# Gated scan attention and an MoE-like feed-forward on one core: attention as closed visits to TensorE, and another start

## The chip, the cores and the metric

The kernel runs on one core of a Trainium2 chip. The metric is the device time of one execution in microseconds. Before the change it is 642.63 us, the median of three runs that lie between 638.91 and 644.26. Engines are named as in the profile: PE is TensorE, DVE VectorE, ACT ScalarE, POOL GpSimd, SP SyncE, which issues all DMAs here (its queue is SPq). PEld is the loading of weights into PE.

## The reference

Four batches of eight heads, 768 positions, head size 48. Each head keeps a complex state of 48 x 48, turned and damped at each position by a gate that is normalised to a magnitude of at most 0.999; what it reads with q is x, 3072 tokens by 384, and x goes through two matrix products with an activation between them:

```python
mag = np.sqrt(a_re * a_re + a_im * a_im)
scale = np.minimum(mag, 0.999) / (mag + 1e-06)
a_re_n, a_im_n = (a_re * scale, a_im * scale)
for t in range(S):
    ar, ai = (a_re_n[:, :, t, :, None], a_im_n[:, :, t, :, None])
    new_re = ar * S_re - ai * S_im
    new_im = ar * S_im + ai * S_re
    kv = np.einsum('bhd,bhe->bhde', k[:, :, t], v[:, :, t])
    S_re, S_im = (new_re + kv, new_im)
    y[:, :, t] = np.einsum('bhd,bhde->bhe', q[:, :, t], S_re)
x = y.transpose(0, 2, 1, 3).reshape(3072, 384)

h = x @ w_in                                   # 384 x 2048
g = np.where(h >= 1, h, np.where(h <= -1, 0.0, (h + 1) ** 2 / 4))
out = g @ w_out                                # 2048 x 384
```

q, k, v and the gates are float32, w_in and w_out are float64.

## The kernel before

**Stages.** The scan is made as attention over chunks: positions are cut into 12 units of 256 (three a batch), each of two chunks of 128. `gates(u)` loads a unit's gates (tile `ai`) and its k and q (`kq`), makes logarithms, angles, sines and decays of them on ACT (one line for all its passes, L396) and DVE, runs a summing scan over the positions on DVE, and ends with two products on DVE, `turn(X, 0)` and `turn(KQ, 1)` (L521), which write k and q turned by the gates into `x` and `kq`. After each turn `spread` moves the result by DMA into the head tiles `hd0`, `hd1`, `hd2` (`hd<-x`, `hd<-kq` at L287), of which there is one set.

`attend(u)` then does, for each chunk and each of two groups of four heads: scores on PE (`sc`, L670), which DVE multiplies by the triangular mask (`am`, L679); transposes of k on PE (`tp`, L613), copied by ACT (`kT`, L624); products of kT with the values on PE (`dp`, L633), added by DVE into the running state (`st`); and values on PE (`yp`, L705 from the state, L713 from the masked scores), copied by ACT into the block's tile `xr` and its rest rows `ys` (L727, L734, L759). After a block's last chunk six DMAs move `ys` into `xr`. In the traces a fp32 matmul is two records.

`moe(blk)` takes two units, 512 tokens, at a time: six blocks. `split` makes `xH` (ACT, L784) and `xL` (DVE, L791) from `xr`, a coarse and a fine part. For each of 16 slices of the hidden size nine matmuls of 512 columns make `h` (L812, in two banks by turns), ACT makes s = Relu(h/2 + 1/2) (L835), DVE g = max(h, s) (L842) and g = min(s, 1) * g (L849), ACT rounds it to `gh` (L855), DVE keeps the difference `gl` (L859), and three slices later nine matmuls add into the three output banks `o0` to `o2` (L872). "MoE" in the texts is all this.

**Weights.** `weights` loads 16 tiles of float64 bits (768 KB each), makes float32 values of them in three integer steps on DVE (L329, L338, L347), casts a coarse part on ACT (L353) and subtracts on DVE for the fine part (L357). Ahead of these ACT sums |w| (L314) and Relu(bound - |w|) (L321) of each tile into `wsum`: the range check. At the end flags are made of all sums; where one fails, another, slow program in the same kernel does the whole work.

**Order.** All steps go into a list with their engine, an estimated cost and what they read and write. `Plan.order` plays the list through with these costs, taking on each engine the ready step with the earliest due time; due times are given to PE steps and outputs and handed back to what feeds them. The kernel's instructions are emitted in the order that comes out, so that each engine, and SP's queue too, works strictly in it. Due times of attention come from `ATTN`, windows inside the MoE of the block before; those of MoE from `FIRST` (the start of MoE) and `STEP` (a slice's time). Attention of units 0 and 1 goes ahead of all MoE and may use the output banks too; that of the others lies in pieces between MoE matmuls, each piece (one group's scores, transposes or values, or the products) with its own due time, in three banks `at0` to `at2` by turns.

Of the kernel before, what the change touches and what calls it, by code (L numbers as in the profile page):

```python
# [10 lines left out]
F32 = mybir.dt.float32  # L11
# [21 lines left out]
T = 512  # L33
NBLK = NB * S // T
UB = T // U

# [15 lines left out]
DMA_FIX, DMA_END, DMA_BW, DMA_ISSUE = 1300, 900, 180.0, 70  # L52
TABLE = 1294
FIRST = 62000
STEP = 5300
PACE = 16 * STEP
LAG = 3
ATTN = ((-24000, -13000), (-12000, -2000), (10000, 38000), (46000, 74000))
# [41 lines left out]
class Plan:  # L100
# [3 lines left out]
    def __init__(self):  # L104
        self.ops = []
        self.slots = {}

# [5 lines left out]
    def op(self, eng, cost, fn, r=(), w=(), due=None, dma=0, after=()):  # L113
        i = len(self.ops)
        pre = set(after)
        split = lambda x: x if isinstance(x, tuple) else (x, None)
# [22 lines left out]
    def order(self):  # L139
# [34 lines left out]
        out = []  # L174
        while done < n:
            best = None
            for e in free:
                if avail[e]:
                    t = free[e]
                elif wait[e]:  # L180
                    t = max(free[e], wait[e][0][0])
                else:
                    continue
                if best is None or t < best[0]:
                    best = (t, e)
            t, e = best
            while wait[e] and wait[e][0][0] <= t:
                _, i = heapq.heappop(wait[e])
                heapq.heappush(avail[e], (due[i], i))
            _, i = heapq.heappop(avail[e])  # L190
# [9 lines left out]
            out.append(i)  # L200
            done += 1
            for s in succ[i]:
                left[s] -= 1
                lat = 0 if (ops[s][0] == eng and not dma) else (0 if dma else LAT[eng])
# [15 lines left out]
def act(n, ptr=False, acc=False, psum=False):  # L220
    return (75 if psum else 93) + (92 if ptr else 0) + (92 if acc else 0) + n * (0.74 if psum else 0.833)
# [6 lines left out]
def per(n):  # L228
    return max(175, n / 2.4 + 3)


# [4 lines left out]
def gated_scan_moe(  # L236
# [20 lines left out]
    ones = c_one  # L257
    fsum = const.tile([P, 2, NU], F32, name="fsum")
# [17 lines left out]
    seen = {}  # L276

# [20 lines left out]
    def weights(kind, i, slot):  # L298
# [9 lines left out]
        acc = lambda q: wsum[:, q, k : k + 1].unsqueeze(1)  # L308
        N = 2 * DM
        pl.op("SP", DMA_ISSUE, lambda: load(k, RAW.get()), w=[RAW], dma=P * N * 8)  # L310
        pl.op(
            "ACT",
            act(N, acc=True),
            lambda: A_.activation(lo, wide(top().bitcast(F32)), AF.Abs, accum_out=acc(0)),  # L314
            r=[RAW],
            w=[part],
        )
        pl.op(
            "ACT",
            act(N, ptr=True, acc=True),  # L320
            lambda: A_.activation(  # L321
                lo, lo.bitcast(F32), AF.Relu, bias=c_tin, scale=-1.0, accum_out=acc(1)
            ),
            w=[part],
        )
# [27 lines left out]
        pl.op("ACT", act(N), lambda: A_.copy(hi, yf()), r=[(RAW, 0)], w=[part])  # L353
        pl.op(
            "DVE",
            dve(N),
            lambda: V_.tensor_tensor(lo, yf(), hi.bitcast(F32), op=ALU.subtract),  # L357
            r=[(RAW, 0)],
            w=[part],
# [6 lines left out]
    def gates(u):  # L366
# [4 lines left out]
        AI = tl(turn_of("g", 4), shape, F32, f"ai_{u}")  # L371
        X = tl(turn_of("g", 4), shape, F32, f"x_{u}")
        KQ = tl(turn_of("g", 4), shape, F32, f"kq_{u}")
        A, I = (lambda: AI.get()[:, :, 0]), (lambda: AI.get()[:, :, 1])
# [4 lines left out]
        if u == 0:  # L379
            for e in range(2):  # L380
                dma(
                    size,
                    lambda e=e: AI.get()[:, :, e],
                    lambda e=e: ari[u, :, :, e],
# [53 lines left out]
        for j in range(NJ):  # L438
            prev = state[:, 0, j : j + 1] if part else 0.0
            ve(  # L440
                66 + U / 0.48,
# [737 lines left out]
```

## Time and profile before

| what | value |
|---|---|
| median of the runs | 642.63 us (638.91 to 644.26) |
| the profiled execution | 642.11 us, of which the span is 640.3 |
| PE busy | 561.1 us (88%), 3298 records |
| PE weight loads | 463.2 us (72%) |
| DVE busy | 470.4 us (73%), 661 |
| ACT busy | 381.4 us (60%), 636 |
| granted TensorE clock, mean | 0.952 |
| HBM read, written | 36.18 MB, 4.72 MB |
| first matmul of MoE | 102.61 us |

An engine's busy time is that of its instructions, without issue and waits. In the rows of groups the columns are line, engine, operation, output and input tiles (without their numbers), shapes and count, and behind the bars busy time with the mean of one in ns, then the idle time of the engine just before them and what ended most of it. In rows in order of time the first two numbers are the start and the length in us, and the bracket tells a wait and what ended it.

### The profile page before, as it was taken

To read this page: it belongs to the slowest core of one execution; us is meant where nothing else is said; L and a number is where in the kernel's file an instruction comes from. 1 tells how busy PE (TensorE), PEld (TensorE's weight loads), DVE (VectorE), ACT (ScalarE), POOL (GpSimd) and SP (SyncE) were. 2 spreads that over 40 slices of the span, in tenths; PEclk is the share of its full clock that TensorE was granted. 3 is DMA by queue.
4 is the path that set the end of the run, shared out by engine and by line. 5 is a ranking of instruction groups with operands and counts; after the bars stand their busy time and mean duration, and the time that the engine had idled before them with its cause. 6 is when DMAs were issued, how large, how long until landed. Compare 5 with 4: busy or idle time off the path is not lost.

```text
span 640.3 us, 8690 instructions
## 1 busy us (share of the span) xinstructions
PE 561.1 (88%) x3298; PEld 463.2 (72%) x3298; DVE 470.4 (73%) x661; ACT 381.4 (60%) x636; POOL 1.4 (0%) x16
## 2 busy tenths in 40 slices
PE   0046396999988999999999999999999999999995
PEld 0045394777866888888788878788888888788884
DVE  2868958999999798878876878887778444545543
ACT  5757677877887866666864566665664323433332
POOL 0000000000000000000000000000000000000000
PEclk9997556999998999999999999999999999999999
DMA  7091927519234416036016045043071050010001
GB/s 270 0 283 44 260 81 182 198 61 296 92 107 96 151 26 198 1 79 205 2 26 197 1 103 181 2 100 123 1 189 45 1 124 2 13 49 1 0 1 55
DMA packets 17697, 61.59 MB, mean 96 GB/s; under 512 B 3632, under 2 KB 4400, under 8 KB 17648
## 3 DMA queue, kind: packets, MB, share of 16 engines
q1 hardware_dynamic: 17648, 60.96, 32.7%
q8 instruction: 28, 0.46, 0.3%
q14 instruction: 21, 0.17, 0.1%
HBM read 36.18 MB, written 4.72 MB: 64 GB/s over the span
## 4 chain that ended last, share of the span: by engine, by line
PE 67%; DVE 20%; ACT 5%; DMA 4%; issue 2%; SPq 1%; DVEq 0%; ACTq 0%
PE o L872 26%; PE h L812 25%; PE sc L670 6%; PE dp L633 3%; PE yp L705 3%; PE yp L713 3%; DMA hd<-x 2%; DVE g L842 2%; PE tp L613 2%; ACT ai L396 1%; DVE gl L859 1%; DVE ai L467 1%; DVE x L521 1%; DMA hd<-kq 1%; DVE g L849 1%
## 5 line engine op out<-in xcount | busy, mean ns | idle before, releaser
L812 PE MATMUL h<-xH,wi 128*128 128x512 f32 x576 | 184.5, 402 | 5.2 <-ACT xH L784 4.3
L872 PE MATMUL o<-gh,wo 128*128 128x512 f32 x576 | 184.6, 402 | 1.8 <-DVE wo L357 1.5
L812 PEld LDWEIGHTS h<-xH,wi 128*128 128x128 f32 x576 | 106.7, 191 | 29.0 <-ACT xH L784 4.7
L872 PEld LDWEIGHTS o<-gh,wo 128*128 128x128 f32 x576 | 104.8, 189 | 25.6 <-issue 3.1
L842 DVE TENSOR_TENSOR g<-h,s 128x512 f32<-128x512 f32 x96 | 65.9, 687 | 74.3 <-ACT s L835 67.5
L812 PE MATMUL h<-xL,wi 128*128 128x512 f32 x288 | 113.9, 395 | 3.1 <-DVE xL L791 3.1
L872 PE MATMUL o<-gl,wo 128*128 128x512 f32 x288 | 113.9, 396 | 2.3 <-DVE gl L859 2.3
L835 ACT ACTIVATE s<-h,cst 128x512 f32<-128x512 f32 x96 | 65.7, 687 | 69.5 <-PE h L812 66.4
L670 PE MATMUL sc<-hd 96*128 96x128 f32 x384 | 58.6, 303 | 53.2 <-DMA hd<-kq 52.3
L855 ACT CAST gh<-g 128x512 fp32r<-128x512 f32 x96 | 59.3, 618 | 67.6 <-DVE g L849 67.5
L670 PEld LDWEIGHTS sc<-hd 96*128 96x128 f32 x384 | 55.4, 214 | 57.5 <-DMA hd<-kq 52.9
L859 DVE TENSOR_TENSOR gl<-g,gh 128x512 fp32r<-128x512 f32 x96 | 65.8, 685 | 21.8 <-ACT gh L855 21.3
L849 DVE SCALAR_TENSOR_TENSOR g<-s,g 128x512 f32<-128x512 f32 x96 | 66.3, 690 | 2.7
L812 PEld LDWEIGHTS h<-xL,wi 128*128 128x128 f32 x288 | 54.8, 190 | 16.6 <-DVE xL L791 4.6
L872 PEld LDWEIGHTS o<-gl,wo 128*128 128x128 f32 x288 | 54.4, 189 | 16.3 <-DVE gl L859 4.3
L396 ACT ACTIVATE ai<-ai 128x768 f32<-128x768 f32 x48 | 40.5, 845 | 23.1 <-DVE ai L487 11.3
L679 DVE TENSOR_TENSOR am<-sc,mask 128x512 f32<-128x512 f32 x48 | 32.6, 685 | 14.8 <-PE sc L670 8.4
L705 PE MATMUL yp<-hd,st 96*64 96x128 f32 x320 | 36.2, 307 | 5.3 <-DVE st L648 4.0
L713 PE MATMUL yp<-am,V 128*64 128x128 f32 x384 | 39.6, 296 | 0.0
L633 PEld LDWEIGHTS dp<-V,kT 128*96 128x96 f32 x320 | 32.3, 176 | 3.6 <-issue 0.8
L633 PE MATMUL dp<-V,kT 128*96 128x48 f32 x320 | 32.6, 258 | 0.9 <-DVE am L679 0.5
L705 PEld LDWEIGHTS yp<-hd,st 96*64 96x64 f32 x320 | 20.0, 148 | 16.3 <-issue 12.2
(76 smaller groups left out, 573.2 us busy)
## 6 DMA issues: line engine op xcount, KB each, us to landing
kq<-in_kq_dram SPq DMA_DIRECT2D x12, 768.0 KB, 5.6
ai<-in_ari_dram SPq DMA_DIRECT2D x11, 768.0 KB, 7.2
hd<-x SPq DMA_DIRECT2D x24, 288.0 KB, 5.1
hd<-kq SPq DMA_DIRECT2D x24, 288.0 KB, 5.5
raw_i<-in_wl_dram SPq DMA_DIRECT2D x8, 768.0 KB, 4.9
raw_o<-in_wl_dram SPq DMA_DIRECT2D x8, 768.0 KB, 4.4
V<-in_v_dram SPq DMA_DIRECT2D x12, 384.0 KB, 3.3
out_dram<-ob SPq DMA_DIRECT2D x18, 256.0 KB, 4.4
```

What stands on the lines that cost most here:

```text
L396: lambda: A_.activation(out(), src(), f, **kw),
L633: PE_.matmul(DP.get()[:, i, :], kT[i // 4].get()[:, i % 4, :], V.get()[:, c, i * D : (i + 1) * D], start=True, stop=True,)
L670: PE_.matmul(SC.get()[:, i, :], t[:, 0, cs], t[:, 1, cs], start=True, stop=True)
L705: PE_.matmul(o, st.get().rearrange("p h e -> p (h e)")[:, lo : lo + 64], head(h)[:, 1, cs], start=True, stop=False,)
L713: PE_.matmul(o, V.get()[:, c, lo : lo + 64], AM.get()[:, 2 * pr + e, :], start=st is None, stop=True,)
L812: PE_.matmul(H.get(), wi[:, f, part, sl], x.get()[:, j, :], start=j == 0 and n == 0, stop=j == NJ - 1 and n == 2,)
L835: lambda: A_.activation(SS.get(), H.get(), AF.Relu, bias=c_half, scale=0.5),
L842: lambda: V_.tensor_tensor(G.get(), H.get(), SS.get(), op=ALU.max),
L849: lambda: V_.scalar_tensor_tensor(G.get(), SS.get(), 1.0, G.get(), op0=ALU.min, op1=ALU.mult),
L855: pl.op("ACT", act(T), lambda: A_.copy(GH.get(), G.get()), r=[G], w=[GH])
L859: lambda: V_.tensor_tensor(GL.get(), G.get(), GH.get().bitcast(F32), op=ALU.subtract),
L872: PE_.matmul(PO[m].get(), wo[:, f, part, sl], g.get(), start=f == 0 and n == 0, stop=f == NF - 1 and n == 2,)
```

## The change

**Closed visits.** `attend` is written anew. Its pieces are grouped into visits to PE, whose pieces follow each other without other matmuls between them: a new argument `glue` of `Plan.op` ties a piece to the one before, and `order` takes a tied piece as soon as its forerunner is placed. The visits of a unit are: scores of chunk 0; transposes of 0; values of 0 with scores of 1; products of 0 with transposes of 1; products of 1 with values of 1 (at a batch's end without the last products and transposes). A visit's first piece waits for the inputs of all its pieces. Values of both groups go into one bank, and two ACT copies a chunk (L808 into `xr`, L815 into `ys`) take the place of four; all six moves of `ys` into `xr` follow the last of them. The windows come from `WINDOW`, `DUR` and `BEGIN`, worked out from a cost model (`moe_time`, `ATTEND`).

**Weights.** The range checks leave `weights`. `ranges(k)` loads each weight tile a second time, late in the kernel, into the gates' tiles and makes the two sums there on ACT. For the first four tiles (`LO_PE`) the fine part is made on PE, as identity times the value minus identity times the coarse part, into the h banks, from which ACT copies it (L409); the first four tiles' loads use four buffers in place of two.

**First block.** In block 0 (`SPARE`) the step min(s, 1) * g is left out on DVE: ACT makes s in three passes, s = Relu(1/2 - h/2), s = Relu(1 - s), s = s * s, and DVE's g = max(h, s) follows. In units 0 to 3 (`ABS_ACT`) an absolute value is made by ACT in place of DVE. The gates `ai` lie as [P, 2, NJ, U] in place of [P, NJ, 2, U], so that each half is contiguous.

**Idle products.** `emit` calls `warm` ahead of each PE step before the first MoE matmul: where the planner left a gap on PE, as many products of the identity and the mask (128 x 128, fp32, results unused) are put there as it reckons to fill it: 181 in eight places. They go into bank `at2`, and once attention has begun into `h1`, unless fine parts of weights are still to come there.

**The rest.** The planner's costs of DMA, ACT and PE steps are changed (DMA 1500 ns and 260 in place of 1300 and 180), `FIRST` is 56000 in place of 62000, and the output tensor is laid out by units, (12, 3, 128, 256), so that a written row has 1 KB in place of 2. Which units make a block does not change.

The PE queue in block 1, before: unit 5's values of chunk 0 (`yp_5_0`, `yp_5_1`), with the MoE's `h` and `o` between them.

```order
L812 MATMUL h_1_11_1990<-xL_1_1409,wi_87 128x512
L705 MATMUL yp_5_0_0_1994<-hd_5_0_1793,st_4_1_1683 64x128
...
L713 MATMUL yp_5_0_0_1994<-am_5_0_0_1886,V_5_1799 64x128 x2
L812 MATMUL h_1_11_1990<-xH_1_1374,wi_87 128x512 x2
...
L872 MATMUL o_1_0_1619<-gl_1_9_1953,wo_88 128x512
L705 MATMUL yp_5_1_0_2021<-hd_5_0_1793,st_4_1_1683 64x128
...
L713 MATMUL yp_5_1_0_2021<-am_5_1_0_1907,V_5_1799 64x128 x2
L872 MATMUL o_1_1_1626<-gh_1_9_1940,wo_88 128x512 x2
```

The two groups' values are two visits with MoE matmuls between them; the scores of chunk 1 are two more, further on. The same place now, after the change:

```order
L984 MATMUL o_1_0_1754<-gl_1_8_2075,wo_90 128x512
L788 MATMUL yp_5_0_2134<-hd_5_0_1910,st_4_1_1924 64x128
...
L796 MATMUL yp_5_0_2134<-am_5_1_0_2069,V_5_1918 64x128 x2
L749 MATMUL sc_5_0_1_2159<-hd_5_0_1910 128x128
...
L749 MATMUL sc_5_1_1_2168<-hd_5_0_1910 128x128
...
L984 MATMUL o_1_1_1760<-gh_1_8_2062,wo_90 128x512 x2
```

Values of both groups and the scores of chunk 1 stand together in one visit. The ACT queue in the start, from the angles of unit 0 on, before: `wi<-raw` are the passes of two tiles' range checks.

```order
L291 ACT_TABLE_LOAD
L396 ACTIVATE ai_0_92<-ai_0_92 128x3x256
L314 ACTIVATE wi_87,wsum_84<-raw_i0_99 128x2x384
L321 ACTIVATE wi_87,wsum_84<-wi_87,cst_74 128x2x384
L396 ACTIVATE ai_0_92<-ai_0_92 128x3x256
L314 ACTIVATE wi_87,wsum_84<-raw_i1_101 128x2x384
L321 ACTIVATE wi_87,wsum_84<-wi_87,cst_74 128x2x384
L396 ACTIVATE ai_0_92<-ai_0_92,cst_74 128x3x256
L291 ACT_TABLE_LOAD
```

Four check passes stand between and around the passes of the gates. Now, from the same table load on:

```order
L334 ACT_TABLE_LOAD
L475 ACTIVATE ai_0_94<-ai_0_94 128x768
L380 CAST wi_89<-raw_i0_101 128x2x384
L409 CAST wi_89<-rest_i0_0_180 128x384
L475 ACTIVATE ai_0_94<-ai_0_94 128x768 x2
L475 ACTIVATE ai_0_94<-ai_0_94,cst_74 128x768
L334 ACT_TABLE_LOAD
L409 CAST wi_89<-rest_i0_1_190 128x384
```

The four check passes are gone from here, and a cast and two copies of a fine part stand in their neighbourhood. On PE, between unit 0's attention and unit 1's scores, there is now:

```order
L394 MATMUL rest_i2_1_417<-raw_i2_109,ident_64 128x384
L395 MATMUL rest_i2_1_417<-wi_89,minus_83 128x384
L1038 MATMUL warm_h1_435<-mask_69,ident_64 128x128 x15
L722 MATMUL dp_0_1_451<-V_0_107,kT_0_0_1_412 96x48 x4
...
L796 MATMUL yp_0_1_461<-am_0_1_1_421,V_0_107 64x128 x2
L1038 MATMUL warm_h1_435<-mask_69,ident_64 128x128 x38
L749 MATMUL sc_1_0_0_563<-hd_1_0_488 128x128
```

Fifteen idle products stand ahead of unit 0's last products, and 38 ahead of unit 1's first scores, where nothing stood before. The core of the diff:

```diff
-FIRST = 62000
+FIRST = 56000
+WINDOW = (0.15, 0.8)
+HOME = 4
+SPARE = 1
+LEAD = 9000
+ABS_ACT = 4
+LO_PE = 4
...
+            nxt = self.glued.get(i)
+            if nxt is not None and not left[nxt]:
+                forced.append(nxt)
...
-    def emit(self):
-        for i in self.order():
+    def emit(self, warm):
+        order = self.order()
+        end = None
+        for i in order:
+            if self.ops[i][0] == "PE":
+                t = self.start[i]
+                gap = LEAD if end is None else t - end
+                warm(i, int((gap - 100) / (2 * 112)))
+                end = t + self.ops[i][1]
             self.ops[i][2]()
...
-            lambda: A_.activation(lo, wide(top().bitcast(F32)), AF.Abs, accum_out=acc(0)),
...
-                lo, lo.bitcast(F32), AF.Relu, bias=c_tin, scale=-1.0, accum_out=acc(1)
...
+            def rest(e=e, R=R):
+                PE_.matmul(R.get(), ident, yf()[:, e], start=True, stop=False)
+                PE_.matmul(R.get(), minus, hi[:, e], start=False, stop=True)
...
+    def ranges(k):
+        RAW = tl(turn_of("g", 4), [P, 2 * DM, 2], U32, f"chk_{k}")
...
+        pl.op("SP", DMA_ISSUE, lambda: load(k, RAW.get()), w=[RAW], dma=P * N * 8)
...
+        def visit(parts):
+            reads = [x for p in parts for x in p[2]]
+            last = None
+            for n, (cost, run, r, psum, tail) in enumerate(parts):
+                cost += 90 if n == len(parts) - 1 else 0
+                last = pl.op("PE", cost, run, r=reads if n == 0 else r, w=[psum], glue=last)
+                visits.append((len(todo_visits), last))
+                kinds[last] = "att"
+                tail()
+            todo_visits.append(0)
...
         for c in range(NC):
-            ams = [scores(g, c) for g in range(2)]
-            states(c)
-            for g in range(2):
-                values(g, c, ams[g])
+            first = [] if pending is None else values(c - 1, *pending)
+            sc, ams = scores(c)
+            visit(first + sc)
+            second = products(c - 1) if c else []
+            pending = (ams, carry.get("st"))
+            if part * NC + c < S // CH - 1:
+                second = second + transposes(c)
+            if second:
+                visit(second)
+            carry["V"] = (V, c)
+        last = values(NC - 1, *pending)
+        if part < NPART - 1:
+            last = products(NC - 1) + last
+        visit(last)
...
+            if spare:
+                pl.op(
+                    "ACT",
+                    act(T, ptr=True),
+                    lambda: A_.activation(SS.get(), SS.get(), AF.Relu, bias=c_one, scale=-1.0),
+                    w=[SS],
+                )
+                pl.op(
+                    "ACT", act(T), lambda: A_.activation(SS.get(), SS.get(), AF.Square), w=[SS]
+                )
...
+            for k in range(NF):
+                ranges(k)
...
+    def warm(i, n):
+        kind = kinds.get(i)
+        if not warmth["over"] and n > 0:
+            slot = "h1" if warmth["att"] else "at2"
+            if slot == "at2" or not warmth["rest"]:
...
+                for _ in range(n):
+                    PE_.matmul(warmth["tile"][slot], ident, mask, start=True, stop=True)
```

More of the change, by code (lines that the diff above doesn't have):

```diff
@@ L111, in tile, with op @@
         return t
-    def op(self, eng, cost, fn, r=(), w=(), due=None, dma=0, after=()):
+    def op(self, eng, cost, fn, r=(), w=(), due=None, dma=0, after=(), glue=None):
         i = len(self.ops)
         pre = set(after)
+        if glue is not None:
+            self.glued[glue] = i
+            pre.add(glue)
         split = lambda x: x if isinstance(x, tuple) else (x, None)
@@ L173, in order @@
         done = 0
-        out = []
+        taken = set()
+        forced = []
         while done < n:
[L176 to L190, printed above, removed]
+            if forced:
+                i = forced.pop()
+                e = ops[i][0]
+                t = max(free[e], ready[i])
+            else:
+                best = None
+                for e in free:
+                    while avail[e] and avail[e][0][1] in taken:
+                        heapq.heappop(avail[e])
+                    while wait[e] and wait[e][0][1] in taken:
+                        heapq.heappop(wait[e])
+                    if avail[e]:
+                        t = free[e]
+                    elif wait[e]:
+                        t = max(free[e], wait[e][0][0])
+                    else:
+                        continue
+                    if best is None or t < best[0]:
+                        best = (t, e)
+                t, e = best
+                while wait[e] and wait[e][0][0] <= t:
+                    _, i = heapq.heappop(wait[e])
+                    if i not in taken:
+                        heapq.heappush(avail[e], (due[i], i))
+                _, i = heapq.heappop(avail[e])
+            taken.add(i)
             eng, cost, _, _, _, dma = ops[i]
@@ L228, in per, with moe_time @@
 def per(n):
-    return max(175, n / 2.4 + 3)
+    return n / 2.4 + 14
+def moe_time(n):
+    return NF * 2 * NJ * 3 * per(n * U)
+ATTEND = 11600
+DUR = [
+    SLACK * (moe_time(len(us)) + ATTEND * (len(BLOCKS[b + 1]) if b + 1 < NBLK else 0))
+    for b, us in enumerate(BLOCKS)
+]
+BEGIN = [FIRST + sum(DUR[:b]) for b in range(NBLK + 1)]
 PLANS = []
@@ L687, in values, with tail, scores, run @@
-        def values(g, c, AM):
+            def tail():
+                if old is None:
+                    fn = lambda: V_.tensor_copy(ST.get(), DP.get())
+                else:
+                    fn = lambda: V_.tensor_tensor(ST.get(), old.get(), DP.get(), op=ALU.add)
+                pl.op("DVE", dve(DM), fn, r=[DP] + ([old] if old else []), w=[ST])
+            return [(NH * pe32(D), run, [*kT, V_c[0]], DP, tail)]
+        def scores(c):
+            cs = slice(c * CH, (c + 1) * CH)
+            out, ams = [], []
+            for g in range(2):
+                SC = bank([P, 4, CH], f"sc_{u}_{g}_{c}")
+                AM = tl(f"am{g}", [P, 4, CH], F32, f"am_{u}_{g}_{c}")
+                def run(g=g, SC=SC):
+                    for i, h in enumerate(GROUPS[g]):
+                        t = head(h)
+                        PE_.matmul(
+                            SC.get()[:, i, :], t[:, 0, cs], t[:, 1, cs], start=True, stop=True
+                        )
+                def tail(SC=SC, AM=AM):
+                    pl.op(
+                        "DVE",
+                        dve(4 * CH),
+                        lambda: V_.tensor_tensor(
+                            AM.get(),
+                            SC.get(),
+                            mask.unsqueeze(1).to_broadcast([P, 4, CH]),
+                            op=ALU.mult,
+                        ),
+                        r=[SC],
+                        w=[AM],
+                    )
+                out.append((4 * pe32(CH), run, [hd[h // 3] for h in GROUPS[g]], SC, tail))
+                ams.append(AM)
+            return out, ams
```

408 lines of the change are left out of this document (207 added, 201 removed).

## The prediction

> **What bounds the kernel now.** I read the span first, then the busy times by stage, then PE in order of time, since one engine is busy nearly all the way. The stretches below are cut at the first matmul of the MoE (102.6 us), at the first of its blocks 1, 2, 4 and 5, and at its last; the columns are PE, PEld, DVE, ACT and POOL busy, the granted TensorE clock, DMA share and GB/s.
>
> ```profile
> span 640.3 us, 8690 instructions
> ```
>
> ```profile
> 0.00:102.60 102.60, 41.73 (x272) 37.92 (x272) 71.58 (x91) 68.06 (x111) 1.37 (x16) 0.78 0.50 159
> 102.60:199.70 97.10, 91.83 (x518) 72.39 (x519) 93.48 (x132) 76.46 (x135) 0.00 (x0) 0.93 0.47 141
> 199.70:298.80 99.10, 96.15 (x594) 79.48 (x593) 82.47 (x117) 67.77 (x108) 0.00 (x0) 1.00 0.41 109
> 298.80:478.40 179.60, 177.36 (x1084) 146.63 (x1082) 141.19 (x201) 112.52 (x187) 0.00 (x0) 1.00 0.32 86
> 478.40:562.80 84.40, 84.16 (x528) 69.51 (x527) 45.98 (x66) 31.67 (x60) 0.00 (x0) 1.00 0.16 43
> 562.80:632.80 70.00, 69.84 (x309) 57.24 (x307) 35.45 (x59) 24.39 (x38) 0.00 (x0) 1.00 0.03 12
> ```
>
> Three regimes: a start in which PE works 42 of 103 us; block 0, where DVE is busy 93.48 of 97.10 and PE is short of work; and the rest, where PE is full. From 102.6 on PE is idle 5.27 + 2.95 + 2.24 + 0.24 + 0.16 = 10.9 us. How much of the other 519.3 is MoE follows from its pitch (nine matmuls a piece in the chain of waits) and its counts:
>
> ```profile
> 229.26 2.04 PE o L872 x9
> 231.31 2.04 PE h L812 x9
> ```
>
> ```profile
> L872 PE MATMUL o<-gh,wo 128*128 128x512 f32 x576 | 184.6, 402 | 1.8 <-DVE wo L357 1.5 <-ACT gh L855 0.3
> L812 PE MATMUL h<-xH,wi 128*128 128x512 f32 x576 | 184.5, 402 | 5.2 <-ACT xH L784 4.3 <-DVE g L842 0.8
> L872 PE MATMUL o<-gl,wo 128*128 128x512 f32 x288 | 113.9, 396 | 2.3 <-DVE gl L859 2.3
> L812 PE MATMUL h<-xL,wi 128*128 128x512 f32 x288 | 113.9, 395 | 3.1 <-DVE xL L791 3.1
> ```
>
> 2.04 / 9 is 0.227 us, and 1728 of them are 392.3 us. So 519.3 - 392.3 = 127.0 us is attention of ten units (20 chunks, about 6.1 us each) and some 5 us of matmuls at half clock. The own time of this execution, 642.11, is its span and 1.8 us. The change leaves the 392.3 alone; it can win in the start, in the 127.0 and in the 10.9.
>
> **Closed visits.** One visit with half a chunk's values, between MoE matmuls:
>
> ```profile
> 265.46 0.39 PE L812 MATMUL h<-xL,wi 128*128 128x512 f32 x1
> 265.78 0.44 PE L705 MATMUL yp<-hd,st 96*64 96x128 f32 x4
> ...
> 266.49 0.39 PE L713 MATMUL yp<-am,V 128*64 128x128 f32 x4
> 266.81 0.73 PE L812 MATMUL h<-xH,wi 128*128 128x512 f32 x2
> 267.38 0.39 PE L812 MATMUL h<-xL,wi 128*128 128x512 f32 x1
> ```
>
> From 265.46 to 267.38 are 1.92 us with three MoE pitches (0.68) in them: the visit costs 1.24. Its four groups follow each other by (266.49 - 265.78) / 3 = 0.24, in all 0.9, so entering and leaving values costs about 0.35. One visit for both halves saves that once a chunk: 20 x 0.35 = 7 us. The scores, transposes and products are the same matmuls; their fewer switches I cost at nothing (by the same reckoning under 0.1 each). A visit takes all three banks at once, so its first part waits for the copies of the last one; in the new order 9 to 30 MoE matmuls (2 to 7 us) lie between two visits inside a unit, which covers a mask of 0.7 us. If that cover goes, each of 50 visits could wait up to a mask, 35 us: an end I hold for unlikely. ACT makes two copies per chunk in place of four; it has room and this counts nothing. But all moves of the rest rows into xr now follow the last copy.
>
> **The start.** PE, then DVE, then SyncE's DMA issues, in order of time:
>
> ```profile
> 45.73 3.67 PE L670 MATMUL sc<-hd 96*128 96x128 f32 x16
> ...
> 74.56 0.80 PE L670 MATMUL sc<-hd 96*128 96x128 f32 x2 [11.61 <-DMA hd<-kq]
> ...
> 97.72 0.64 PE L713 MATMUL yp<-am,V 128*64 128x128 f32 x4
> 102.61 1.22 PE L812 MATMUL h<-xH,wi 128*128 128x512 f32 x2 [4.26 <-ACT xH L784]
> ...
> 119.22 1.95 PE L670 MATMUL sc<-hd 96*128 96x128 f32 x16
> ```
>
> ```profile
> 0.00:66.70 66.70, 18.12 (x128) 16.73 (x128) 44.34 (x56) 42.35 (x66) 1.37 (x16) 0.93 0.47 156
> 80.00:90.00 10.00, 10.00 (x66) 9.26 (x64) 5.51 (x9) 7.00 (x12) 0.00 (x0) 0.50 0.31 127
> ```
>
> ```profile
> 50.51 1.29 DVE L679 TENSOR_TENSOR am<-sc,mask 128x512 f32<-128x512 f32 x2 [3.88 <-PE yp L713]
> 64.94 1.76 DVE L521 TENSOR_TENSOR kq<-kq,ai 128x1536 f32<-128x1536 f32 x1
> ```
>
> ```profile
> 64.93 4.00 SPq L287 DMA_DIRECT2D hd<-x  x5
> 94.23 3.67 SPq L287 DMA_DIRECT2D xr<-ys  x6
> ```
>
> The last product of unit 1's gates ends at 66.7, up to which DVE worked 44.3 us; the head moves start at 64.93, scores at 74.56 (9.6 later), attention ends at 98.36, MoE starts at 102.61. Sixteen score matmuls take 3.67 us here and 1.95 later: all of unit 1's attention runs at half clock (0.50 in the stretch 80 to 90).
>
> ```profile
> L314 ACT ACTIVATE wi<-raw_i 128x768 fp32r<-128x768 f32 x8 | 7.2, 899 | 0.0
> L314 ACT ACTIVATION_READ_ACCUMULATOR wi<-raw_i 128x1 f32 x8 | 1.5, 189 | 0.0
> L321 ACT ACTIVATE wi<-wi,cst 128x768 fp32r<-128x768 f32 x8 | 7.5, 936 | 0.2
> L624 ACT COPY kT<-tp 128x384 f32<-128x384 f32 x40 | 18.3, 478 | 14.6 <-PE tp L613 14.5
> L835 ACT ACTIVATE s<-h,cst 128x512 f32<-128x512 f32 x96 | 65.7, 687 | 69.5 <-PE h L812 66.4 <-DVE gl L859 1.6 <-DMA out_dram<-ob 0.6
> L849 DVE SCALAR_TENSOR_TENSOR g<-s,g 128x512 f32<-128x512 f32 x96 | 66.3, 690 | 2.7
> L503 DVE TENSOR_SCALAR ai<-ai 128x768 uint32<-128x768 uint32 x12 | 8.3, 689 | 2.6 <-ACT ai L396 2.4
> L329 DVE TENSOR_SCALAR y_i<-raw_i 128x768 uint32<-128x768 uint32 x8 | 4.4, 550 | 0.0
> ```
>
> A weight tile's range check is 0.90 + 0.94 + two reads of 0.19 = 2.2 us of ACT. Four stood ahead of unit 1's last product: 8.8 go. Against them come seven copies of low parts from PSUM (0.48 each by the kT copy, 3.3), two Abs and two more casts (about 0.9 each, 3.5): ACT gains 2 us. DVE has six more weight steps and two subtractions fewer ahead of that product (3.0 more), two sign masks fewer (1.4) and four shorter contiguous steps (0.69 to 0.55 by the two rows: 0.5): 1.1 more. The 3.88 wait goes, since a chunk's masks now stand behind the scans. So the product ends near 66.7 + 1.1 - 3.9 - 2 = 62 (66.7 + 1.1 = 68 if every wait stays).
>
> The head tiles are single: their refill also waits for unit 0's last visit, and that for a kT copy behind a table load on ACT. I put it at 62.5, scores at 62.5 + 9.6 = 72. Thirty-eight idle products before them are 76 records of 0.12, 9 us: they fit that wait. At full clock the 23.8 us of attention become half and 1.5 of waits, 13.5, to 86. Then two copies (0.7), six moves (3.67 to issue, about 2 to land), one cast (0.6) and ACT's table load in front (1.3): 9 us, where before it were 4.25. MoE starts at 95 instead of 102.6. Bounds: 90 if ACT and DVE wait for nothing new, 105 if the clock stays at half.
>
> [...]
>
> **Block 0.** DVE loses sixteen steps of 0.69 (11.0), two sign masks (1.4) and 0.6 by contiguity: 93.5 becomes 80.5, while PE needs 288 x 0.227 = 65.4 and four chunks, about 89. ACT loses nine checks (19.8) and gains two passes of at most 0.69 for each of sixteen steps (22.0) and two Abs (1.7): 76.5 becomes 80. Nothing is saturated any more but PE, with two engines at 90%. Of the 10.9 us idle I take 6 away, and 4 of the 5 at half clock, since these follow the gaps. Ends: nothing, or all 16.
>
> **The checks at the end.** Sixteen reloads of 768 KB and 35 us of ACT fall, by the order, in the block before the last, where ACT was busy 31.7 of 84.4: hidden. Uncovered, a check of 1.1 us ahead of s could hold sixteen steps, 18 us; two banks for h give each about 4 us, so I count 0 (to +4).
>
> **The end.** From the last matmul to the end of the span are 640.3 - 632.8 = 7.5. Output rows of half the length I put at +0.5 (0 to 2).
>
> Sum: 95 + 392.3 + (127.0 - 7 - 4 = 116) + (10.9 - 6 = 5) + 8 = 616.3 span, and 1.8: **618 us**.
>
> **Rivals.**
> 1. The clock falls again in unit 1's attention, or the idle products run at half clock and are themselves waited for. For it: 0.50 over a busy stretch. Against: PE keeps 1.00 in every later stretch with attention in it. MoE starts at 105: 628 us.
> 2. Block 0 stays bound by DVE and ACT, in order and both near 90%; the 10 us taken there stay: 628. Both together: 638, no change.
> 3. All goes better: MoE at 90, no idle time in block 0: 607.
> 4. Slower, in block 0: h's bank is now held through three ACT steps and one DVE step, 4 x 0.69, and each can stand behind a foreign step (0.9 to 1.8) of an engine that works in order. PE needs the bank back after some 7 us (three pieces of 2.04 and its share of attention). Held for 8 it costs 16 us; from 9.0 on, 2 us a step, 32 us, the time passes 648; at 9.3: 655. Against: queues at 90% seldom add more than one step each.
> 5. The checks' loads land late and ACT waits in order: +8, 626.
>
> **How the numbers follow.** Forecast 0.60, rival 1 0.13, rival 2 0.09, both 0.04, rival 3 0.06, rival 4 0.04, rival 5 0.04. One per cent (6.4 us) is about what a measurement of this kernel can tell. Faster by more: all but "both" and rival 4, less a little for rivals 1 and 2 running long: 0.90; same 0.06; slower 0.04. The range takes in rivals 1, 2, 5 and most of 3: 605 to 632.
>
> **What would show it.** MoE's first matmul near 95 and the clock at 1.00 in the attention before it; about 50 visits of attention after that; DVE near 80 us in block 0 and PE's idle time from there on near 5; ACT's checks in the block before the last without PE waiting. The forecast is wrong if MoE starts after 100, if block 0 takes more than 95 us, or if PE waits for copies within a visit.

## The result, and the profile after

The changed kernel takes 623.87 us, the median of four runs (620.05 to 625.76); the kernel before takes 642.74 in the same comparison. The ratio is 0.971, with a 95% interval of 0.9645 to 0.977. The profiled execution took 623.92 us, 622.1 of them its span. The same stretches as before (PE, PEld, DVE, ACT and POOL busy, clock, DMA share, GB/s), cut at the first MoE matmul, at the first of blocks 1, 2, 4 and 5, and at the last MoE matmul's end:

```profile
span 622.1 us, 9454 instructions
```

```profile
0.00:93.84 93.84, 78.64 (x659) 72.80 (x659) 73.03 (x93) 62.20 (x91) 1.36 (x16) 0.91 0.56 183
93.84:184.76 90.92, 86.34 (x519) 71.86 (x519) 77.78 (x109) 74.48 (x117) 0.00 (x0) 0.96 0.50 148
184.76:282.61 97.85, 94.08 (x578) 78.69 (x578) 79.32 (x115) 64.56 (x101) 0.00 (x0) 0.98 0.42 109
282.61:457.86 175.25, 173.62 (x1080) 146.19 (x1079) 137.37 (x196) 107.69 (x170) 0.00 (x0) 1.00 0.31 84
457.86:546.36 88.50, 87.73 (x553) 74.01 (x552) 48.36 (x69) 60.89 (x119) 0.00 (x0) 1.00 0.57 186
546.36:614.77 68.41, 68.41 (x303) 56.11 (x301) 34.83 (x58) 23.68 (x37) 0.00 (x0) 1.00 0.04 12
```

MoE starts 8.8 us earlier, its stretch (first to last matmul) is 520.9 us in place of 530.2, and what lies behind it is 7.3 in place of 7.5. From the first MoE matmul on, PE is idle 4.58 + 3.77 + 1.63 + 0.77 + 0 = 10.75 us, nearly as much as before (10.9). The 392.3 us of MoE at full pace and this idle time leave 117.9 us for attention and half clock, where before there were 127.0.

The start on PE, in order of time:

```profile
55.22 5.95 PE L1038 MATMUL warm_h<-mask,ident 128*128 128x128 f32 x30 [5.49 <-ACT wi L409]
61.00 1.48 PE L722 MATMUL dp<-V,kT 128*96 128x48 f32 x16
...
64.33 8.75 PE L1038 MATMUL warm_h<-mask,ident 128*128 128x128 f32 x76
72.91 1.95 PE L749 MATMUL sc<-hd 96*128 96x128 f32 x16
...
85.57 7.41 PE L1038 MATMUL warm_h<-mask,ident 128*128 128x128 f32 x64
93.84 0.73 PE L909 MATMUL h<-xH,wi 128*128 128x512 f32 x2 [0.85 <-ACT xH L879]
...
101.54 0.79 PE L749 MATMUL sc<-hd 96*128 96x128 f32 x2 [2.73 <-DMA hd<-kq]
102.89 3.36 PE L749 MATMUL sc<-hd 96*128 96x128 f32 x14 [0.56 <-DMA hd<-kq]
```

Unit 1's scores now run at full clock (1.95 us for 16 records, where eight of them took 1.97 to 2.08), and its attention takes 72.91 to 85.64, 12.7 us in place of 23.8. But 15 idle products (30 records) take 5.95 us, and unit 0's last products stand behind them. And soon after MoE has begun PE waits again, for unit 2's heads. The longest waits of PE from MoE's start on (waiting operation, what ended the wait, us in all, times, longest):

```profile
PE h L909 <- DVE g L953: 4.5, 5, 1.7
PE sc L749 <- DMA hd<-kq: 3.3, 2, 2.7
PE o L984 <- ACT gh L967: 1.8, 2, 1.4
```

Why unit 2's heads are late is read from SyncE's issues and from ACT:

```profile
87.32 1.28 ACT L334 ACT_TABLE_LOAD   x1
88.61 0.48 ACT L808 COPY xr<-yp 128x384 f32<-128x384 f32 x1
```

```profile
89.28 3.67 SPq L330 DMA_DIRECT2D xr<-ys  x6
93.06 3.85 SPq L330 DMA_DIRECT2D hd<-x  x5
97.03 4.07 SPq L330 DMA_DIRECT2D hd<-kq  x5
```

Unit 1's last values end at 85.64, but their copies stand behind passes of the gates and a table load on ACT and end at 89.3; then 16 moves go out of one queue, 0.6 to 0.8 us each, until 101.1.

### The profile page after: what moved, and what is told of

Its sections match the earlier page's. It is cut to its first block, busy times and chain, and to the rows that moved or that the text cites. A ratio compares the mean times of both kernels' runs of the same rounds, so it can differ in the third digit from the quotient of the medians.

```text
span 622.1 us, 9454 instructions
## 1 busy us (share of the span) xinstructions
PE 589.0 (95%) x3684; PEld 499.7 (80%) x3684; DVE 451.0 (72%) x637; ACT 394.1 (63%) x633; POOL 1.4 (0%) x16
## 4 chain that ended last, share of the span: by engine, by line
PE 52%; DVE 20%; ACT 13%; DMA 8%; issue 3%; SPq 3%; ACTq 0%; DVEq 0%
PE o L984 20%; PE h L909 20%; PE sc L749 4%; ACT ai L475 4%; SPq L330 3%; ACT x L475 3%; PE dp L722 3%; DVE ai L546 2%; PE yp L788 2%; PE yp L796 2%; DVE g L953 2%; ACT L334 2%; DVE x L521 2%; DMA hd<-kq 2%; DMA ai<-in_ari_dram 1%
## 5 line engine op out<-in xcount | busy, mean ns | idle before, releaser
L909 PE MATMUL h<-xH,wi 128*128 128x512 f32 x576 | 182.1, 397 | 5.4 <-DVE g L953 4.5
L984 PE MATMUL o<-gh,wo 128*128 128x512 f32 x576 | 179.7, 393 | 1.8 <-ACT gh L967 1.8
L475 ACT ACTIVATE ai<-ai 128x768 f32<-128x768 f32 x52 | 43.7, 844 | 38.4 <-DVE ai L566 18.6
L909 PEld LDWEIGHTS h<-xL,wi 128*128 128x128 f32 x288 | 54.2, 188 | 13.5 <-DVE xL L886 1.7
L961 DVE SCALAR_TENSOR_TENSOR g<-s,g 128x512 f32<-128x512 f32 x80 | 55.4, 692 | 2.7
L749 PE MATMUL sc<-hd 96*128 96x128 f32 x384 | 51.4, 289 | 3.8 <-DMA hd<-kq 3.3
L749 PEld LDWEIGHTS sc<-hd 96*128 96x128 f32 x384 | 48.5, 201 | 7.7 <-DMA hd<-kq 4.3
L796 PE MATMUL yp<-am,V 128*64 128x128 f32 x384 | 35.5, 273 | 0.0
L475 ACT ACTIVATE x<-x 128x768 f32<-128x768 f32 x24 | 20.3, 844 | 18.9 <-DVE x L521 16.4
L788 PE MATMUL yp<-hd,st 96*64 96x128 f32 x320 | 32.1, 278 | 0.0
L722 PEld LDWEIGHTS dp<-V,kT 128*96 128x96 f32 x320 | 30.0, 165 | 1.9 <-ACT kT L703 0.2
```

Of the source, the lines that this page charges most:

```text
L475: lambda: A_.activation(out(), src(), f, **kw),
L722: PE_.matmul(DP.get()[:, i, :], kT[i // 4].get()[:, i % 4, :], V_c[0].get()[:, V_c[1], i * D : (i + 1) * D], start=True, stop=True,)
L749: PE_.matmul(SC.get()[:, i, :], t[:, 0, cs], t[:, 1, cs], start=True, stop=True)
L788: PE_.matmul(o, st.get().rearrange("p h e -> p (h e)")[:, lo : lo + 64], head(h)[:, 1, cs], start=True, stop=False,)
L796: PE_.matmul(o, V.get()[:, c, lo : lo + 64], ams[g].get()[:, 2 * pr + e, :], start=st is None, stop=True,)
L909: PE_.matmul(H.get(), wi[:, f, part, sl], x.get()[:, j, :], start=j == 0 and n == 0, stop=j == NJ - 1 and n == 2,)
```

## The experiments

**The idle products.** Once all are left out, once the 15 ahead of unit 0's last products alone, and once the kernel before gets some.

```diff
-        if not warmth["over"] and n > 0:
+        if False:
```

> The changed kernel without its idle products. Theory (the idle products hold the clock up in unit 1's attention, but the 15 ahead of unit 0's last products stand in the way of these): unit 0's last visit ends near 62 in place of 64.3, scores of unit 1 at about 70, its attention at half clock 22 us in place of 12.7, MoE starts at 99 to 101 in place of 93.8, whole time about 630. Rival A (the clock comes back by itself as soon as PE is busy, so the idle products only stand in the way): MoE starts at 91 to 92, whole time about 621. Rival B (the idle products are the whole gain of the start): MoE starts at 102 or later, 633 or more.

Measured: 618.71 us (617.95 to 620.29), ratio to the kernel before 0.964 (0.960 to 0.968): 5.2 us less than the changed kernel with its idle products. PE in order of time, and stretches of it:

```profile
67.55 0.77 PE L749 MATMUL sc<-hd 96*128 96x128 f32 x2 [6.07 <-DMA hd<-kq]
68.95 3.33 PE L749 MATMUL sc<-hd 96*128 96x128 f32 x14 [0.64 <-DMA hd<-kq]
...
92.24 1.22 PE L909 MATMUL h<-xH,wi 128*128 128x512 f32 x2 [6.85 <-ACT xH L879]
```

```profile
77.00:78.00 1.00, 1.00 (x6) 0.90 (x5) 0.55 (x1) 0.65 (x2) 0.00 (x0) 0.50 0.95 393
78.00:79.00 1.00, 1.00 (x10) 1.00 (x10) 0.24 (x1) 0.00 (x0) 0.00 (x0) 0.95 0.91 367
```

Unit 1's scores begin 5.4 us earlier, run at half clock, and the clock comes back by itself at 78.0, 10.5 us after they began. So attention takes 17.8 us, ends at 85.38 all the same (85.64 with the idle products), and MoE starts at 92.24. My theory falls: it had the half clock lasting for all of unit 1's attention. Rival A has the sign and nearly the size, though the clock came back after 10.5 us and not as soon as PE was busy.

```diff
-        if not warmth["over"] and n > 0:
+        if not warmth["over"] and n > 0 and n != 15:
```

> The changed kernel without the 15 idle products ahead of unit 0's last products alone; the 38, 3 and 32 after them stay. Theory (these 15 ran at half clock when the products' inputs were there already): unit 0's last visit ends at 61 to 62 in place of 64.3, scores of unit 1 at 70.5 in place of 72.9, MoE starts at 91 to 92 in place of 93.8, whole time about 621.5. Rival (the start is bound by DVE and ACT, and PE only waits elsewhere): MoE starts at 93.5 to 94.5, no change.

```profile
59.83 9.09 PE L1038 MATMUL warm_h<-mask,ident 128*128 128x128 f32 x76
68.76 1.95 PE L749 MATMUL sc<-hd 96*128 96x128 f32 x16
...
88.53 0.73 PE L909 MATMUL h<-xH,wi 128*128 128x512 f32 x2
```

Measured: 617.23 us (616.82 to 619.24), ratio 0.962 (0.958 to 0.9665), 6.6 us less than the changed kernel. Unit 0's last visit ends at 59.90 in place of 64.39, scores begin 4.15 us earlier, and MoE starts at 88.53, 5.3 us earlier: more than the theory's 2. The 15 were a loss. The other 166 bring the start of MoE 3.7 us forward (88.53, where it is 92.24 with none). What they bring to the whole can't be told: with none at all the time is 1.5 us longer, and the runs of the two overlap.

```diff
+    def warm(i):
+        if unit1 and i in unit1:
+            unit1.clear()
+            t = ps.tile([P, P], F32, tag="h1", name="warm", bufs=1)
+            for _ in range(45):
+                PE_.matmul(t, ident, mask, start=True, stop=True)
```

> The kernel before with one thing added: 45 idle products ahead of unit 1's first scores, in the 11.6 us that PE waits there. Theory A (the half clock of unit 1's attention cost about 10 us of the start): its 23.8 us fall to 13 to 15, MoE starts at 93 to 95 in place of 102.6, whole time 632 to 635. Theory B (as in the changed kernel, where leaving the idle products out cost nothing: DVE, ACT and the moves set the start): MoE starts at 98 to 102, whole time 638 to 643.

```profile
62.98 10.28 PE L580 MATMUL warm<-mask,ident 128*128 128x128 f32 x90
75.52 0.49 PE L680 MATMUL sc<-hd 96*128 96x128 f32 x2 [2.26 <-DMA hd<-kq]
...
97.09 1.22 PE L824 MATMUL h<-xH,wi 128*128 128x512 f32 x2 [4.75 <-ACT xH L796]
101.61 0.80 PE L824 MATMUL h<-xL,wi 128*128 128x512 f32 x1 [3.30 <-DVE xL L803]
```

Measured: 642.5 us, ratio 0.9985 (0.9966 to 1.0005), no change. Unit 1's attention falls to 16.8 us and MoE starts at 97.09 in place of 102.61, but the first fine part of x comes 4.5 us after that, since DVE has two turns of 1.76 us and a weight step of 0.95 ahead of it, and the stretch of MoE grows from 530.2 to 535.5 us: the 5.5 us are given back, 1.5 of them before block 1 and the rest bit by bit after it. The earlier start of MoE was worth nothing here, where DVE didn't follow.

**The visits.** First every piece a visit of its own again, with values still in one piece; then the values alone cut in two.

```diff
-            visit(first + sc)
+            for p in first + sc:
+                visit([p])
...
-                visit(second)
+                for p in second:
+                    visit([p])
...
-        visit(last)
+        for p in last:
+            visit([p])
```

> The changed kernel with every piece a visit of its own again (values of both groups still one piece in one bank): 96 visits after the first MoE matmul in place of 50. Theory (only entering and leaving values costs, about 0.3 us each, and their number stays the same): the stretch from the first to the last MoE matmul stays within 2 us of its 520.9. Rival (each visit costs, at the 0.17 us that the changed kernel's visits without waits show above their matmuls): 46 more visits, 8 us more.

A visit of four scores alone, in this run, and one of all values of a chunk:

```profile
236.11 0.39 PE L912 MATMUL h<-xL,wi 128*128 128x512 f32 x1
236.34 1.05 PE L749 MATMUL sc<-hd 96*128 96x128 f32 x8
237.15 0.70 PE L912 MATMUL h<-xH,wi 128*128 128x512 f32 x2
237.70 0.40 PE L912 MATMUL h<-xL,wi 128*128 128x512 f32 x1
```

```profile
220.38 0.39 PE L987 MATMUL o<-gl,wo 128*128 128x512 f32 x1
...
222.61 0.73 PE L912 MATMUL h<-xH,wi 128*128 128x512 f32 x2
223.18 0.39 PE L912 MATMUL h<-xL,wi 128*128 128x512 f32 x1
```

From 236.11 to 237.70 are 1.59 us with three MoE pitches (0.68) in them: 0.91 for eight records, 0.114 each, where 16 records in one go take 1.95 / 16 = 0.12. So a visit of scores of its own costs next to nothing. By the same reckoning all values in one visit cost 223.18 - 220.38 - 0.68 = 2.12 us. All the same the run takes 629.54 us (ratio 0.981, 0.977 to 0.9855), 5.7 more than the changed kernel: MoE starts at 95.59 (+1.8) and its stretch is 523.8 (+2.9), 0.9 beyond what the theory allowed. PE's idle time in this stretch is no longer than in the changed kernel (10.5 and 10.75 us), so what the stretch gained is busy time: 3.1 us, at most 0.07 for each of the 46 further visits. The rival's 0.17 us per visit falls, but closing visits does save PE a little. In the start the planner places the open pieces and the idle products otherwise, too; which of them makes the 1.8 us isn't shown.

```diff
-            return [((16 if st else 8) * 110 + 400, run, r, YP, tail)]
+            for g in range(2):
+                rr = [ams[g], V, *(hd[h // 3] for h in GROUPS[g])] + ([st] if st else [])
+                out.append(
+                    (
+                        (8 if st else 4) * 110 + 200,
+                        lambda g=g: run(g),
+                        rr,
+                        (YP, g),
+                        tail if g else (lambda: None),
+                    )
+                )
+            return out
...
-            visit(first + sc)
+            if first and u > 1:
+                visit(first[:1])
+                first = first[1:]
+            visit(first + sc)
...
-        visit(last)
+        if u > 1:
+            visit(last[:-1])
+            last = last[-1:]
+        visit(last)
```

> The changed kernel with the values of the two groups in two visits again from unit 2 on (still one bank and two copies a chunk): 64 visits in place of 50, 20 more entries into values. Theory (0.24 to 0.33 us for each): the stretch from the first to the last MoE matmul grows by 5 to 6.5 us, whole time about 629. Rival (the halves cost no more than the whole, since the cost goes with the matmuls): no change.

```profile
249.71 0.39 PE L1000 MATMUL o<-gl,wo 128*128 128x512 f32 x1
250.03 0.44 PE L787 MATMUL yp<-hd,st 96*64 96x128 f32 x4
...
251.06 0.73 PE L1000 MATMUL o<-gh,wo 128*128 128x512 f32 x2
251.63 0.40 PE L1000 MATMUL o<-gl,wo 128*128 128x512 f32 x1
```

```profile
PE h L925 <- DVE g L969: 6.8, 4, 4.2
```

Measured: 636.85 us, ratio 0.991 (0.988 to 0.994), 13.0 more than the changed kernel. From 249.71 to 251.63 are 1.92 us with 0.68 of MoE: half the values cost 1.24, of which their matmuls are 0.9, exactly as in the kernel before. So the price of 0.33 to 0.35 for each entry holds, and 20 more entries would be 6.6 to 7 us. The stretch grew by 12.6 (520.9 to 533.5), twice the theory's 5 to 6.5. Of these, 2.9 are longer waits (PE is idle for 13.6 us), the longest 4.2 us for g, 17 us into block 1. And PE was busy at half clock for 17.3 us of the stretch by the clock records, where it was 9.2, which by estimate costs about 4, half of the 8.1 more. That leaves 5.7 for the 20 entries. MoE starts at 92.20 here, 1.6 earlier than in the changed kernel, with the same order on PE before it: by so much two executions of the same start can differ.

**Block 0 and the range checks.** The change in block 0's gate undone, the checks put back where they were, both, and the checks left out:

```diff
-SPARE = 1
+SPARE = 0
```

> The changed kernel with block 0's gate as in the other blocks (DVE makes min(s, 1) * g, ACT one pass). Sixteen steps of 0.69 go back to DVE, whose 77.8 us in block 0 become 89, and ACT's 74.5 become 53. Theory (block 0 was bound by DVE before the change): the time from the first h of block 0 to that of block 1 grows from 90.9 to 95 to 98, whole time 628 to 631. Rival (the gain of block 0 came from the weight checks that left ACT, and DVE at 89 still fits): 90 to 92, whole time within 2 us of the changed kernel's.

```diff
+        pl.op(
+            "ACT",
+            act(N, acc=True) + 50,
+            lambda: A_.activation(lo, wide(top().bitcast(F32)), AF.Abs, accum_out=acc(0)),
+            r=[RAW],
+            w=[part],
+        )
+        pl.op(
+            "ACT",
+            act(N, ptr=True, acc=True) + 50,
+            lambda: A_.activation(
+                lo, lo.bitcast(F32), AF.Relu, bias=c_tin, scale=-1.0, accum_out=acc(1)
+            ),
+            w=[part],
+        )
...
-            for k in range(NF):
-                ranges(k)
+            pass
```

> The changed kernel with the range checks back in the making of the weights, and no second loads. ACT gets 8.8 us more ahead of unit 1's turned k and q and 20 us more in block 0 (74.5 to 94). Theory (the checks on ACT held up the start before): MoE starts at 97 to 100 in place of 93.8 and block 0 takes 97 to 100 in place of 90.9, whole time 634 to 640. Rival A (the start waits for unit 0's last products on PE, not for ACT): MoE starts within 1 us of 93.8, block 0 alone grows, 630 to 633. Rival B (ACT has room for the checks everywhere): no change.

The third run has both edits:

> The changed kernel with both undone at once: range checks back in the making of the weights, and block 0's gate as in the other blocks. Each alone left block 0 at 89.4 and 90.5 us. Theory A (either relief is enough, both together bring back the old bound on DVE and ACT): block 0 takes 95 to 97, whole time 633 to 636. Theory B (block 0 was never bound by DVE's work; its 97.1 us came from waits at its end and the half clock after them, which go with the new order): block 0 at 89 to 91, whole time 627 to 630, as with the checks alone.

Block 0 in the three runs, from its first h to that of block 1. Gate undone:

```profile
92.34:182.86 90.52, 86.36 (x518) 71.87 (x519) 82.94 (x120) 56.45 (x88) 0.00 (x0) 0.96 0.47 142
```

Checks in front:

```profile
97.82:187.26 89.44, 85.35 (x519) 71.14 (x519) 75.65 (x107) 83.92 (x143) 0.00 (x0) 0.98 0.49 143
```

Both:

```profile
98.36:188.81 90.45, 85.14 (x520) 71.08 (x519) 83.61 (x121) 69.48 (x116) 0.00 (x0) 0.98 0.48 145
```

The times are 624.8 (ratio 0.972, 0.970 to 0.9745), 628.09 (0.977, 0.975 to 0.979) and 627.68 us (0.977, 0.975 to 0.978). Block 0 takes 89.4 to 90.5 us in all of them, with DVE busy 75.7 or 83.6 and ACT 56.5 or 83.9: at these loads neither engine's work bounded it, and the new gate of block 0 brought nothing measurable. The checks cost in the start alone, where the theory put 3 to 6 us: the last turned k and q end at 60.6 in place of 57.05, MoE starts at 97.8 in place of 93.84, and the whole is 4.2 us longer. The planner places the idle products otherwise in the two runs with the checks in front (11 in place of 15 ahead of unit 0's last products), so the 4 us are not the checks' alone.

```diff
-            for k in range(NF):
-                ranges(k)
+            pl.op("DVE", 100, lambda: V_.memset(wsum, 0.0))
```

> The changed kernel without any range check of the weights (the 16 second loads of 768 KB and ACT's 32 passes over them are left out; nothing else is). Theory (they are hidden in the block before the last): time within 1.5 us of the changed kernel, block 4 88.5 us as with them. Rival (ACT's 35 us hold s steps up, or the loads delay head moves): block 4 shorter by 2 to 4 us, whole time 620 to 622.

Measured: 623.37 us (ratio 0.969, 0.966 to 0.971). The 16 loads and ACT's 36.5 us late in the kernel are hidden:

```profile
L430 ACT ACTIVATE chk<-chk,cst 128x768 f32<-128x768 f32 x16 | 16.0, 997 | 0.3
L422 ACT ACTIVATE chk<-chk 128x768 f32<-128x768 f32 x16 | 14.5, 906 | 2.9 <-DMA chk<-in_wl_dram 2.8
```

These are the changed kernel's groups of the two passes, 30.5 us; the reads of the sums, 6 us, come on top.

**Fine parts of the weights on PE**, undone:

```diff
-LO_PE = 4
+LO_PE = 0
```

> The changed kernel with the fine parts of all weight tiles on DVE (no products of the identity with the weights, no copies of them on ACT). ACT loses eight copies of 0.48 (3.8 us), DVE gets four subtractions of 0.95 in the start. Theory (DVE leads up to unit 1's turned k and q): the last of these ends 2 to 4 us later than at 57.1; as unit 0's last products wait for ACT and the idle products until 61, MoE still starts at 93 to 95, whole time within 2 us of 624. Rival (the copies on ACT stand in front of the kT copy that unit 0's last products wait for): MoE starts at 90 to 92, whole time 620 to 622.

Measured: 622.88 us (ratio 0.969, 0.967 to 0.971), no difference that can be told. DVE's last turn ends at 60.26 in place of 57.05, as the theory had it, but unit 0's last visit ends at 58.03 in place of 64.39, as the rival had it; MoE starts at 92.70, later than the rival's 90 to 92. The rival's reason isn't shown by it: in this run the planner also puts 11 idle products in place of 15 ahead of unit 0's last products, and they run at full clock (22 records in 2.65 us).

**Two further versions.** Unit 2's scores moved behind the first product into the output banks, without the 15 idle products:

```diff
+                first = [o0[0]] if u == 2 else []
                 last = pl.op(
-                    "PE", cost, run, r=reads if n == 0 else r, w=[psum], glue=last)
+                    "PE", cost, run, r=reads if n == 0 else r, w=[psum], glue=last, after=first
+                )
...
+        if u == 2:
+            w0, w1 = w0 + 6000, w1 + 2000
```

> The changed kernel without the 15 idle products, and with unit 2's first scores behind the first product into the output banks (30 MoE matmuls after the start of MoE in place of 18). Theory (in the run without the 15, unit 2's scores cost 5.7 us above their matmuls, as they wait for head moves that SyncE issues behind the moves of the rest rows, and run cold after it): this goes, block 0 falls from 89.8 to 85 or 86, whole time about 613. Rival (block 0 is bound by DVE and ACT in any case): block 0 stays at 89 to 90, whole time about 617.

```profile
PE h L915 <- DVE g L959: 7.4, 6, 2.3
```

Measured: 618.07 us (ratio 0.961, 0.959 to 0.963). The wait for the heads is gone, but h waits longer for g (7.4 us in place of 4.2; in block 0 alone 5.2 in place of 0.3), and block 0 takes 90.7 us where it took 89.8 without the move. The rival's numbers came: the wait for heads lay over one for g, which shows once the other is gone. Whether DVE's load or only the order of its steps makes g late isn't shown; DVE was busy 79.0 of the 90.7 us.

Then ACT's copies of unit 1's last values ahead of the table load, without the 15 idle products, and 25 in place of 32 ahead of MoE:

```diff
-            table("natural_log_exp_and_others")
+            table("natural_log_exp_and_others", copied if u == 3 else ())
```

> The changed kernel without the 15 idle products, with 25 in place of 32 ahead of MoE, and with ACT's copies of the last values of unit 1 ahead of a table load that stood before them. Theory (the copies set the start of MoE, through the moves of the rest rows): against the run without the 15 alone MoE starts 0.5 to 1.5 us earlier than 88.5, whole time 615.5 to 617. Rival (DVE's turned k and q or the head moves set it): 88.5 and 617.

Measured: 616.34 us (615.34 to 617.80), ratio 0.9585 (0.9565 to 0.9605), the lowest median of all runs. MoE starts at 88.33, only 0.2 earlier. One pass of the gates came ahead of the copies instead, so they end only 0.4 earlier, and the table load, a cast and two passes now stand between them and xH on ACT. Against the run without the 15 alone (617.23) it is the same within the spread.

## Why the prediction was right, and where it was not

The direction, the range (605 to 632) and nearly the size hold: 618 forecast, 623.87 measured, 18.9 us less where 24.6 were forecast. Term by term, on the profiled execution:

| term | forecast | measured |
|---|---|---|
| MoE starts | 95 | 93.84 |
| MoE at full pace | 392.3 | 392.3 (taken as such) |
| attention and half clock after that | 116 | 117.9 |
| PE idle after that | 5 | 10.75 |
| behind the last matmul | 8 | 7.3 |
| span | 616.3 | 622.1 |

**The step that failed** is "of the 10.9 us idle I take 6 away". It rested on the reading that block 0 is short of work because DVE is full (93.48 of 97.10). DVE did fall as forecast (80.5 forecast, 77.8 measured; ACT 80 and 74.5). Before the change, all but 0.3 us of PE's waits in block 0 ended with a step of DVE:

```profile
PE h L812 <- DVE xL L791: 1.7, 1, 1.7
PE o L872 <- DVE gl L859: 1.7, 3, 1.0
PE o L872 <- DVE wo L357: 1.5, 1, 1.5
```

Of these 4.9 us 1.3 are left after the change (g 1.0, xL 0.3). But 3.3 us of waits for unit 2's heads came in their place, so PE's idle time in block 0 went only from 5.27 to 4.58 us; with DVE's sixteen steps back it is 4.16, so the gate's steps did nothing for it. The heads wait behind six moves in SyncE's queue. PE asks for them 5.0 us after the start of MoE (98.81), where the first scores behind it stood 16.6 us after it (119.22); that was not in the sum. With that wait moved out of the way 5.2 us of waits for g stood there instead. And behind block 0, where the sum had some of the 6 us too, the idle time went from 5.6 to 6.2. An engine at 96% of a stretch was taken for its bound; the 5.27 us of PE's idle time in the same row said how little there was to win. No run gives DVE its 93.5 us back (83.6 at most), so what it would do at that load stays open.

Block 0 still fell by 6.2 us, and it did so with gate and checks as before too (90.45). Where from I have only by accounting: on PE, the times between neighbouring MoE matmuls above 0.227 us sum to some 15 us in block 0 before and 4 after, waits and half-clock stretches at its start and end among them. No run takes that apart further.

**Half clock, "4 of the 5",** failed as well. By the clock column 0.07 of block 0's 97.1 us were lost before, 6.8 us; after the change it is 0.04 of 90.9 and 0.02 of the next 97.9, 5.6 us. So about 1 us was won, and of the 9.1 us by which attention and half clock shrank some 8 are attention's, where 7 were forecast. That 117.9 lies near 116 is luck: two misses stand against each other.

**Closed visits, 7 us.** The price is confirmed: half the values in a visit of their own cost 1.24 us in the run with halves, and all of them in one 2.12 in the run with open visits, so joining them saves 2 x 1.24 - 2.12 = 0.36 a chunk, 7.2 us in 20. (The prediction's own sum has a slip: four groups at 0.24 are 0.95, not 0.9, and would leave 0.29 for the entry.) For scores it is confirmed that a visit more costs next to nothing (0.114 us a record alone, 0.12 together); for transposes and products the run with open visits gives only the bound of 0.07 for a visit of any kind.

**The start.** Its size is right (95 and 93.84), the reasons only in part. The last turn ends at 57.05, where 62 were forecast with bounds of 62 and 68. The scores begin at 72.91 (72 forecast) for another reason: unit 0's last visit ended at 64.39, behind 15 idle products at a clock of 0.57. This is the second half of rival 1, "the idle products run at half clock and are themselves waited for", and the part on the start spoke only of the 38. Attention at full clock took 12.7 us (13.5 forecast), and the way from its end to MoE 8.2 (9 forecast, though the parts that the prediction lists add up to 8.3). So that 95 is near 93.84 is in part luck: the last turn came 5 us earlier than forecast, and unit 0's last visit took that back. The row at 45.73 that the prediction gives as unit 1's scores at half clock is unit 0's; unit 1's own rows show the same pace. Nor did the start gain from the idle products as they stood: without any MoE starts at 92.24, 1.6 us earlier. Those that stand well bring it 3.7 us forward, and the 15 take 5.3 back. In the kernel before idle products gain 5.5 us at the start of MoE and nothing in the end. With the checks back the start loses 4 of the 8.8 us. The rest isn't isolated by a run: with the checks back the last turn still ends at 60.6 in place of 66.7.

**The checks at the end** cost 0, as counted. **The end** cost nothing either (7.3 and 7.5). Rival 4 didn't come: h's bank is waited for 4.5 us in the whole kernel. In all, the runs show some 7 us of the 18.9 for the joined values and up to 4 for the checks; the rest is not taken apart.

## What to carry to other kernels

Before an engine is taken for a stage's bound because it is busy there, look at how long the engine that sets the time is idle in the same stretch: that, not the busy share, is what can be won, and another wait may lie under the one that goes. Filler work in a queue that works in order is safe only behind everything that is needed soon (here 15 idle products ahead of unit 0's last products brought MoE 5.3 us later); where a planner sizes it from its own guess of a gap, look at what stands behind it. And price a switch between kinds of work by kind: here entering values costs a third of a microsecond (0.33 to 0.35) and entering scores next to nothing (0.114 us a record in a visit alone, 0.12 in one go), so joining the one pays and joining the other hardly does.

## What the runs showed that was not expected

How long PE stays at half clock once it is busy again differs much. In the run without idle products scores begin at 67.55 after a wait of 6.07 us, and the clock is 0.50 up to 78.0: 10.5 us. In the kernel before it stayed at 0.50 from the scores at 74.56 to the end of attention at 98.36, though PE was busy nearly all that time. In the kernel before with idle products the clock fell 1.6 us after the second of two waits (2.26 and 1.02 us), and was back 3.4 us later:

```profile
78.00:79.00 1.00, 1.00 (x11) 1.00 (x9) 1.00 (x2) 0.00 (x0) 0.00 (x0) 0.79 0.93 184
...
81.00:82.00 1.00, 1.00 (x12) 0.77 (x8) 0.00 (x0) 1.00 (x1) 0.00 (x0) 0.50 1.00 397
82.00:83.00 1.00, 1.00 (x10) 0.92 (x8) 0.00 (x0) 0.99 (x3) 0.00 (x0) 1.00 0.97 393
```

What makes the difference is open. By the clock records the stretches at half clock last 6.83, 44.37 and 6.83 us in the trace of the kernel before (from 53.85, 64.09 and 190.38) and 10.24, 6.83, 6.83 and 3.41 us in that of the changed kernel (from 15.76, 53.31, 101.10 and 278.59); one more in each begins behind the last matmul of MoE, at 637.53 and 619.92. For a prediction it means that the end of a half-clock stretch can't be placed from one trace: that of the kernel before showed 24 us, and with another order of the same work it was 10.

The clock column has a gap too. In the kernel before, the 16 scores at 45.73 take 3.67 us, twice the 1.95 of later, yet the column reads 1.00 from 40 to 50 us: the first change of the clock that the trace recorded is at 53.85. Ahead of that, the pace of the matmuls has to tell.
